# A fused layer norm, attention and gated MLP on one core: loading all x tiles at once, two tiles' statistics on ScalarE, and a last query group in two halves

## The chip, the core and the metric

The kernel runs on one core of one Trainium2 chip. Its metric is the device time of one execution in microseconds (us); the time before is the median of three runs. A further execution was taken by the hardware profiler, and its page and trace are what is read here. TensorE is called PE, VectorE DVE, ScalarE ACT, GpSimd POOL and SyncE SP. PEld is TensorE's weight load, which overlaps its matmuls.

## The reference

With x of 2048 rows and 1024 columns (bf16), 32 heads of 32 columns, and an MLP of 3584 hidden columns:

```python
xn = _layernorm(x)
qkv = (xn @ wqkv)                      # split into q, k, v of 32 heads
p = softmax(q k^T * 32 ** -0.5)        # per head, 2048 x 2048
s = (p v) @ wo
y = _layernorm(xn)
h = gelu_tanh(y @ w1 + b1)
g = silu(h @ w2 + b2)
out = x + s * g
```

## The kernel before

All work is described as operations for the five engines (PE, ACT, DVE, POOL, SP). A planner on the host (class _Plan) runs an event simulation with a cost for each operation, and so fixes, before launch, the order in which each engine takes its instructions. On the chip every engine takes its list in order and waits on semaphores. Priorities (the number at the end of a dve or act call, lower first), positions and due times of the dense PE work decide the planner's choices. ACT, DVE and PE are strictly in the planned order, so an instruction that waits holds up all that is behind it on its engine.

**Stages.** The rows of x are 16 tiles of 128. In the prologue each tile is loaded (load_x, L626), its mean and variance are computed, POOL raises the variance to the power -0.5 (L794), and DVE normalises it into one of four buffers (normalize, L748). Statistics are two BATCH_NORM_STATS2 (L785) and an aggregate (L787) on DVE, but for tile AT = 1, whose two passes (a copy and a square, each with an accumulator) run on ACT (L769) with three small DVE operations behind them. Tiles 0 to 3 are transposed on PE (tr_item, L733) and copied by ACT into xnT (L737); tiles 4 to 15 are transposed by DMA (L752). The first ten x tiles are loaded at once into buffers in hT; the other six follow when buffers come free (load_x with first[2n-5], L783).

From xnT the queries, keys and values of head group 0 are projected (q_item, k_item, v_item, at L617 as all plain matmuls). Query and key results of 256 columns are copied out of PSUM by DVE (L712) and by ACT (L722). Where PE has nothing else it runs idle matmuls on an identity (filler, L668).

**Attention.** There are eight head groups of four heads and eight query groups of 256 queries (qb) for each. A unit is one query group against 256 keys (kp): eight score matmuls for four heads side by side (L846) into four PSUM banks, then two exponentials of 128 x 1024 on ACT (L855) into a P buffer, of which there are ten in the steady state. Three pairs of banks serve the scores in turn. Value products (v_fn) and sums over keys are PE matmuls of 32 columns by 256 (L612); to save PE work DVE first adds P tiles pairwise (tree, pair_add: L872, L886) and PE sums the result with a matrix of ones. The quotient (L941 to L950) transposes the sums in blocks of 32, takes reciprocals, transposes them back, and multiplies the values.

**MLP.** In parallel, chunk after chunk of 256 rows: y is normalised and transposed by DMA, multiplied by w1 (L617, DVE adds the bias at L1022), then a gelu built from five DVE operations (L1034 to L1039, priority 3) and one tanh on ACT (L1037) over four hidden tiles at a time, then w2 (L617), a silu (tanh on ACT, L1064) and a store of g. The w2 items of a chunk start when the gelus they read are done.

**Ending.** In the last head group (own, w = HG - 1) each query group is followed by its output product with wo: per tile of 128 rows two pieces of 512 columns, eight accumulating matmuls each, then DVE multiplies by g (L1269) and adds x (L1272) and SP stores (L1299). For the last query group (late) the first seven of the eight matmuls run early (items in the queue "last"), DVE prepares xf from them (L1277, L1280), and after the quotient only the last matmul remains (items in lates, queue "fin"): piece 0 is finished on DVE (L1290, L1293), pieces 1 to 3 by a copy on ACT (L1285), a multiply and an add on DVE (L1287, L1293), and each is stored by itself (L1295).

```python
timing(pv, us, qb == NQB - 1)
quotient(pv, g, OTr[:, w, qb * 256:(qb + 1) * 256], [("OTr", w, qb)], dead, qb == NQB - 1, 0.5)
```

## Time and profile before

| What | Before |
|---|---|
| median of three runs | 1038.02 us (1036.59 to 1038.26) |
| the profiled execution | 1038.8 us, of which the span is 1037.0 us |
| mean granted TensorE clock | 0.998 |
| busy, share of the span | PE 97%, PEld 62%, DVE 91%, ACT 98%, POOL 1% |
| exponentials (L855) | 1004 records of 1024, 937.4 us busy, mean 1236 ns |
| DMA | 162 GB/s mean over the span, 167.99 MB |

The span runs from the first to the last instruction of the profiled execution; its time holds 1.8 us more, which lie around the span. Durations overlap where instructions are pipelined: an exponential lasts more than 1 us in its record and yet one begins every 0.92 us. Some matmul and activation records are missing. In the listings a line holds the start, the duration of the group, engine, source line, operation, output and inputs, the count, and in brackets the idle time before it with what ended it.

### The profile page before, as it was taken

What the parts mean: (1) busy time and instruction counts of PE and PEld (TensorE: products, weight loads), DVE (VectorE), ACT (ScalarE), POOL (GpSimd) and SP (SyncE); (2) the same over time, 40 slices, a digit from 0 to 9 for tenths busy, and PEclk for the clock granted to TensorE, in tenths of its full rate; (3) what the DMA queues carried; (4) which work ended last, traced back from release to release, by engine and by line L of the source; (5) the groups of instructions that cost most, each with busy time, mean ns of one, the idle gap of its engine ahead of it and who ended that gap; (6) DMA issues with size and microseconds to landing.
All of it is one profiled execution on the core that took longest, in us unless ns stands there. A gap on an engine that the chain in (4) does not pass through costs nothing.

```text
span 1037.0 us, 31480 instructions
## 1 busy us (share of the span) xinstructions
PE 1000.8 (97%) x14096; PEld 638.6 (62%) x14161; DVE 940.6 (91%) x1308; ACT 1017.2 (98%) x1094; POOL 11.5 (1%) x21
## 2 busy tenths in 40 slices
PE   8999999999999999999999999999999999899997
PEld 6656557666766567666666676666666665664443
DVE  7658999999889999997899989998999889877898
ACT  6999999999999999999999999999999999999996
POOL 2200000000000000000000000000000000000000
PEclk9999999999999999999999999999999999999999
DMA  7994655635665658456447576565365762784421
GB/s 204 166 234 118 173 166 165 191 108 147 192 186 167 168 152 227 129 147 194 136 129 189 146 215 172 159 179 161 104 160 161 212 175 70 230 249 137 135 79 52
DMA packets 318199, 167.99 MB, mean 162 GB/s; under 512 B 56688, under 2 KB 306032, under 8 KB 318064
## 3 DMA queue, kind: packets, MB, share of 16 engines
q1 hardware_dynamic: 318064, 165.98, 58.0%
q8 instruction: 111, 1.82, 0.8%
q14 instruction: 24, 0.20, 0.1%
HBM read 146.55 MB, written 12.06 MB: 153 GB/s over the span
## 4 chain that ended last, share of the span: by engine, by line
ACT 85%; PE 10%; DMA 2%; DVE 2%; issue 1%; SPq 0%; POOL 0%
ACT P L855 78%; PE ps L617 6%; ACT ut L1037 5%; PE ps L612 3%; PE ps L846 2%; DMA xnT<-gw 1%; ACT gw L1064 1%; DMA w2r<-in_B_w_dram 1%; DVE stats L785 1%; DMA hT<-in_A_x_dram 0%; DVE gw L748 0%; DVE hT L1293 0%; DVE V L690 0%; DVE hT L1287 0%; DVE mv L787 0%
## 5 line engine op out<-in xcount | busy, mean ns | idle before, releaser
L855 ACT ACTIVATE P<-ps 128x1024 bf16<-128x1024 f32 x1004 | 937.4, 1236 | 3.6 <-PE ps L846 3.4
L872 DVE TENSOR_TENSOR PA<-P 128x2048 bf16<-128x2048 bf16 x175 | 212.3, 1216 | 38.3 <-ACT P L855 37.7
L617 PE MATMUL ps<-yT,w1r 128*128 128x256 bf16 x1792 | 228.5, 273 | 1.0 <-DVE hT L1022 0.7
L617 PE MATMUL ps<-w2r,hT 128*128 128x256 bf16 x1792 | 223.2, 273 | 0.5 <-DMA w2r<-in_B_w_dram 0.2
L846 PE MATMUL ps<-QKT 32*128 32x256 bf16 x4096 | 203.3, 273 | 13.8 <-ACT P L855 10.9
L886 DVE TENSOR_TENSOR PR<-PR,PA 128x2048 bf16<-128x2048 bf16 x175 | 211.6, 1210 | 1.2
L617 PEld LDWEIGHTS ps<-yT,w1r 128*128 128x128 bf16 x1792 | 164.1, 98 | 54.5 <-issue 29.3
L617 PEld LDWEIGHTS ps<-w2r,hT 128*128 128x128 bf16 x1792 | 163.4, 98 | 50.0 <-issue 31.3
L846 PEld LDWEIGHTS ps<-QKT 32*128 32x128 bf16 x4096 | 60.7, 92 | 144.3 <-ACT P L855 137.3
L612 PE MATMUL ps<-P,V 128*32 128x256 bf16 x4016 | 137.2, 274 | 0.3 <-issue 0.3
L617 PE MATMUL ps<-xnT,wqk 128*128 128x512 bf16 (+1 forms) x511 | 119.1, 360 | 6.5 <-DMA xnT<-gw 2.4
L612 PEld LDWEIGHTS ps<-P,V 128*32 128x32 bf16 x4016 | 95.0, 96 | 31.8 <-issue 22.5
L617 PE MATMUL ps<-wv,xnT 128*128 128x256 bf16 (+1 forms) x576 | 87.1, 285 | 0.5 <-DMA xnT<-gw 0.2
L617 PEld LDWEIGHTS ps<-xnT,wqk 128*128 128x128 bf16 x560 | 49.6, 98 | 53.3 <-issue 14.1
L1022 DVE TENSOR_TENSOR hT<-ps,b1T 128x512 bf16<-128x512 f32 x112 | 76.5, 683 | 1.8 <-PE ps L617 1.1
L872 DVE TENSOR_TENSOR PR<-P 128x2048 bf16<-128x2048 bf16 x61 | 74.1, 1214 | 0.4 <-ACT P L855 0.2
L617 PEld LDWEIGHTS ps<-wv,xnT 128*128 128x128 bf16 x576 | 52.4, 98 | 24.1 <-issue 11.4
L1037 ACT ACTIVATE ut<-ut 128x2048 bf16<-128x2048 bf16 (+1 forms) x32 | 61.0, 1906 | 0.0
L702 DVE CAST QKT<-ps 128x512 bf16<-128x512 f32 x58 | 39.6, 683 | 1.3 <-PE ps L617 0.9
L941 DVE STREAM_TRANSPOSE nt<-ps 128x256 f32<-128x256 f32 x64 | 28.4, 443 | 12.7 <-PE ps L612 12.5
L1039 DVE TENSOR_TENSOR hT<-ut,hT 128x2048 bf16<-128x2048 bf16 (+1 forms) x32 | 34.5, 1079 | 0.2
L1034 DVE TENSOR_TENSOR ut<-hT 128x2048 bf16<-128x2048 bf16 (+1 forms) x32 | 34.5, 1079 | 0.1
(96 smaller groups left out, 549.5 us busy)
## 6 DMA issues: line engine op xcount, KB each, us to landing
w1r<-in_B_w_dram SPq DMA_DIRECT2D x112, 512.0 KB, 4.2
w2r<-in_B_w_dram SPq DMA_DIRECT2D x128, 448.0 KB, 4.6
hT<-in_A_x_dram SPq DMA_DIRECT2D x20, 256.0 KB, 3.9
wqk<-in_A_wqkv_dram SPq DMA_DIRECT2D x16, 256.0 KB, 3.9
yst<-in_A_x_dram SPq DMA_DIRECT2D x16, 256.0 KB, 4.4
g_scratch<-gw SPq DMA_DIRECT2D x32, 128.0 KB, 3.9
o_scratch<-ot SPq DMA_DIRECT2D x56, 64.0 KB, 3.4
xnT<-o_scratch SPq DMA_DIRECT2D x7, 512.0 KB, 6.6
```

Of the source, the lines that this page charges most:

```text
L612: ins = e.matmul(dst(j), lhsT=lhsT(j), rhs=rhs(j), start=start, stop=stop, tile_position=(0, 32 * j), skip_group_check=True)
L617: return e.matmul(dst, lhsT=lhsT, rhs=rhs, start=start, stop=stop, skip_group_check=True)
L702: dve(lambda e: e.tensor_copy(QKT[sl][:, which, tq * 512:(tq + 1) * 512], bank(it.bank)), c_ps(512), [], [(nm, sl, 2 * tq), (nm, sl, 2 * t ...
L846: ins = e.matmul(bank(b0[j], kk * 256, (kk + 1) * 256), lhsT=QKT[sl][32 * j:32 * j + 32, 1, kb * 128:(kb + 1) * 128], rhs=QKT[sl][32 * j:3 ...
L855: x = act(lambda e, h=h: e.activation(Pt[pi][:, 2 * h:2 * h + 2].rearrange("p j k q -> p (j k q)"), ps[:, pr[h] * 1024:(pr[h] + 1) * 1024] ...
L872: return dve(lambda e: e.tensor_tensor(dst[:].rearrange("p u j q -> p (u j) q"), src[:].rearrange("p u j k q -> p (u j) k q")[:, :, 0, :], ...
L886: return dve(lambda e: e.tensor_tensor(fl3(pr), fl3(pr), fl3(PA[i]), op=ALU.add), c_b16(2048), [("PA", i), tok], [tok], 3.2)
L941: dve(lambda e: e.transpose(nt_t[:], bank(pv.bank, 256, 512)), c_ps(256) + 120, [], [("nt",)], prio, pv)
L1022: dve(lambda e: e.tensor_tensor(hT[:, hs], bank(it.bank).rearrange("p (k t) -> p k t", k=2), b1T[:, 2 * pi:2 * pi + 2].unsqueeze(2).to_bro ...
L1034: dve(lambda e: e.tensor_tensor(u_, x_, x_, op=ALU.mult), c_b16(n), hs_, [("ut", ui)], 3)
L1037: act(lambda e: e.activation(u_, u_, ACT.Tanh, scale=GC), c_acts(n), [("ut", ui)], [("ut", ui)], 1)
L1039: dve(lambda e: e.tensor_tensor(x_, u_, x_, op=ALU.mult), c_b16(n), [("ut", ui)] + hs_, hs_, 3)
```

## The change

The change has two parts.

In the prologue all sixteen x tiles are loaded at once, the last six into buffers of the trees (PR) and of the MLP's input (yst); so the K weights of head group 1 and the first y tiles are loaded after the last tile's normalisation instead of after tile 9's and 11's. AT becomes (1, 3): tile 3's statistics run on ACT as well. The first queries and keys are projected for tile 0 and tile 1 separately (qk_first), into two banks at once, and tile 3's keys apart from tile 2's.

In the ending the last query group of the last head group is cut into two halves of 128 queries (half_unit: four units of 512 keys for each half, the same size of exponential; sums straight from P on PE, no tree; half_quotient). The output pieces of the first half are queued ahead (firsts, queue "fin0"), those of the second half stay last (lates). Query group 6 also takes its first seven output matmuls early. The gelu of the last MLP chunk is cut finer and gets higher priorities on DVE (1.4) and ACT (-1), the queries of the last head group are placed later, and the planner may run a transposition of the prologue between the matmuls of another item.

```diff
+            if use is None and S["do"] is not None and th < len(tq) and tq[th].chunks[0].left == 0 and tq[th].chunks[0].ready <= t:
+                heads["tr"] += 1
+                tq[th].k = 1
+                S["mode"] = "d"
+                commit(tq[th].chunks[0], t)
+                return
...
-        NTR, NWARM, NG0, AT = 4, 8, 3, 1
+        NTR, NWARM, NG0, AT = 4, 8, 3, (1, 3)
...
+        for i in range(2):
+            pr_flat = PR[i][:].rearrange("p u j q -> p (u j q)")
+            xst += [pr_flat[:, 0:1024], pr_flat[:, 1024:2048]]
+        xst += [yst_t[i][:] for i in range(2)]
...
-        for t in range(4, NXS):
+        for t in range(NTR, NT):
             load_x(t)
         load_v(0)
...
+            for lo, w in ((0, 128), (128, 128)) if n < 2 else ((0, 256),):
+                for dc in range(DC):
+                    def fn(e, b, dc=dc, lo=lo, w=w):
+                        at = n * 256 + lo
+                        return mm(e, bank(b, lo, lo + w), wqk[wk0][:, dc, :], xnT[:, dc, at:at + w], dc == 0 and lo == 0, dc == DC - 1)
+                    chunk(it, fn, Q256 if w == 256 else Q128, [("xnT", 2 * n + i, dc) for i in range(lo // 128, (lo + w) // 128)] + [("wqk", wk0)])
...
+        def qk_first():
+            it = _Item("pro", -0.001)
+            for lo, d0, d1 in ((0, 0, 8), (128, 0, 4), (128, 4, 8)):
+                for k, wi in ((0, wq0), (1, wk0)):
+                    for dc in range(d0, d1):
+                        def fn(e, b, dc=dc, lo=lo, k=k, wi=wi):
+                            return mm(e, bank(k or b, lo, lo + 128), wqk[wi][:, dc, :], xnT[:, dc, lo:lo + 128],
+                                      dc == 0 and lo == 0, dc == DC - 1)
+                        chunk(it, fn, Q128, [("xnT", lo // 128, dc), ("wqk", wi)], [("S", 0, 1)] if k else ())
+            dve(lambda e: e.tensor_copy(QKT[0][:, 0, 0:256], bank(it.bank, 0, 256)), c_ps(256), [], [("Q", 0, 0)], 0, it)
+            act(lambda e: e.activation(QKT[0][:, 1, 0:256], bank(1, 0, 256), ACT.Copy), c_act(256), [("S", 0, 1)], [("K", 0, 0)], -1)
...
+                if ts[0] in AT:
+                    a_ = ts[0]
                     for k, f, sc in ((0, ACT.Copy, 1.0 / D), (1, ACT.Square, D ** -0.5)):
-                        act(lambda e, k=k, f=f, sc=sc: e.activation(
-                            fl3(PA[0])[:, k * 1024:(k + 1) * 1024], xst[AT], f, scale=sc, accum_out=mv[:, AT, k:k + 1]),
-                            c_acts(1024) + 93, [XS(AT)], [("st", AT, k)], 1)
-                    dve(lambda e: e.tensor_tensor(lnp[:, AT:AT + 1, 2], mv[:, AT:AT + 1, 0], mv[:, AT:AT + 1, 0], op=ALU.mult), 65,
-                        [("st", AT, 0)], [("s2",)], 0.95)
-                    dve(lambda e: e.scalar_tensor_tensor(lnp[:, AT:AT + 1, 0], mv[:, AT:AT + 1, 1], EPS, lnp[:, AT:AT + 1, 2], op0=ALU.add,
-                                                         op1=ALU.subtract), 65,
-                        [("st", AT, 1), ("s2",)], [("ve", AT)], 0.95)
-                    dve(lambda e: e.tensor_tensor(mv[:, AT:AT + 1, 1], mv[:, AT:AT + 1, 1], lnp[:, AT:AT + 1, 2], op=ALU.subtract), 65,
-                        [("st", AT, 1), ("s2",)], [("mv", AT)], 1.1)
+                        act(lambda e, k=k, f=f, sc=sc, a_=a_: e.activation(
+                            fl3(PA[a_ // 2])[:, k * 1024:(k + 1) * 1024], xst[a_], f, scale=sc, accum_out=mv[:, a_, k:k + 1]),
+                            c_acts(1024) + 93, [XS(a_)], [("st", a_, k)], 1)
...
-                    if t >= NXS:
-                        load_x(t, [first[2 * n - 5]])
...
+            if n == 0:
+                pro_q.append(qk_first())
+            else:
+                if n < NG0:
+                    pro_q.append(q_item(n))
+                pro_q.append(k_item(n))
...
-            wk = load_qk(hg, 1, [first[9]] if hg == 1 else ())
+            wk = load_qk(hg, 1, [first[NT - 1]] if hg == 1 else ())
             wq = load_qk(hg, 0)
...
-            lst += [(x, "q", t) for t, x in enumerate((42, 46, 50, 54) if hg == HG - 1 else (42, 58, 72, 86))]
+            lst += [(x, "q", t) for t, x in enumerate((50, 52, 54, 56) if hg == HG - 1 else (42, 58, 72, 86))]
...
-                    [("yst", t2)], rate=390.0, extra=[first[11]] if c == 0 else ())
+                    [("yst", t2)], rate=390.0)
...
+            half = c == NCH - 1 and pi in (NW1 - 3, NW1 - 1)
+            if p % 4 != 3 and pi != NW1 - 1 and not (pi == 1 and c % 2) and not half:
                 return it
-            k = 2 if (pi == NW1 - 1 and p % 4 != 3) or (pi == 1 and c % 2) else 4
+            k = 2 if (pi == NW1 - 1 and p % 4 != 3) or (pi == 1 and c % 2) or half else 4
...
+            gp, ga = (1.4, -1) if c == NCH - 1 and pi >= 5 else (3, 1)
+            dve(lambda e: e.tensor_tensor(u_, x_, x_, op=ALU.mult), c_b16(n), hs_, [("ut", ui)], gp)
+            dve(lambda e: e.tensor_scalar(u_, u_, GA, 1.0, op0=ALU.mult, op1=ALU.add), c_b4(n), [("ut", ui)], [("ut", ui)], gp)
+            dve(lambda e: e.tensor_tensor(u_, u_, x_, op=ALU.mult), c_b16(n), [("ut", ui)] + hs_, [("ut", ui)], gp)
+            act(lambda e: e.activation(u_, u_, ACT.Tanh, scale=GC), c_acts(n), [("ut", ui)], [("ut", ui)], ga)
+            dve(lambda e: e.tensor_scalar_add(u_, u_, 1.0), c_b4(n), [("ut", ui)], [("ut", ui)], gp)
+            dve(lambda e: e.tensor_tensor(x_, u_, x_, op=ALU.mult), c_b16(n), [("ut", ui)] + hs_, hs_, gp)
...
+        for i in range(2):
+            after([("PR", i)], [XS(10 + 2 * i), XS(11 + 2 * i)])
+            after([("yst", i)], [XS(14 + i)])
...
+        def half_unit(hg, qb, a, kq, pv):
+            n = unit_n["n"]
+            unit_n["n"] += 1
+            sl, vs = hg % 2, vslot[hg]
+            m = slot_n["n"]
+            slot_n["n"] += 1
+            pi = (m - 16) % NP
+            b0 = [(4 * n + j) % 6 for j in range(4)]
+            q0 = qb * 256 + a * 128
+
+            def s_fn(e):
+                for kk in range(4):
+                    kb = 4 * kq + kk
+                    for j in range(4):
+                        ins = e.matmul(bank(b0[j], kk * 128, (kk + 1) * 128),
+                                       lhsT=QKT[sl][32 * j:32 * j + 32, 1, kb * 128:(kb + 1) * 128],
+                                       rhs=QKT[sl][32 * j:32 * j + 32, 0, q0:q0 + 128],
+                                       start=True, stop=True, tile_position=(32 * j, 0), skip_group_check=True)
+                return ins
+            pr = [b0[0] // 2, b0[2] // 2]
+            o = add("PE", s_fn, 300.0, 210, [("Q", sl, qb), ("K", sl, 2 * kq), ("K", sl, 2 * kq + 1)],
+                    [("S", k, h) for k in pr for h in range(2)])
+            plan.s_queue.append(o)
+            for h in range(2):
+                x = act(lambda e, h=h: e.activation(Pt[pi][:, 2 * h:2 * h + 2].rearrange("p j k q -> p (j k q)"),
+                                                    ps[:, pr[h] * 1024:(pr[h] + 1) * 1024], ACT.Exp, scale=SCALE),
+                        c_act(1024), [("S", pr[h], 0), ("S", pr[h], 1)], [("P", pi, h)], 0)
+            Ph = Pt[pi].rearrange("p j k (i q) -> p j (k i) q", i=2)
+
+            def v_fn(e):
+                for kk in range(4):
+                    ins = quad(e, lambda j: bankp(pv.bank, j, 0, 128), lambda j: V[:, vs, 4 * kq + kk, 32 * j:32 * j + 32],
+                               lambda j: Ph[:, j, kk, :], kq == 0 and kk == 0, False)
+                return ins
+
+            def o_fn(e):
+                for kk in range(4):
+                    ins = quad(e, lambda j: bankp(pv.bank, j, 256, 384), lambda j: ones[:], lambda j: Ph[:, j, kk, :], False, False)
+                return ins
+            ks = [("P", pi, 0), ("P", pi, 1)]
+            vc = add("PE", v_fn, 4 * Q128, TL, ks + [("V", vs, 2 * kq), ("V", vs, 2 * kq + 1)], [], item=pv)
+            oc = add("PE", o_fn, 4 * Q128, TL, ks + [("ones",)], [], item=pv)
+            return x, vc, oc
...
+        def half_quotient(pv, dst, W, extra, copied=False):
+            pq_ = -0.5 if copied else -2
+            if copied:
+                dve(lambda e: e.tensor_copy(nv_t[1][:, 0:128], bank(pv.bank, 0, 128)), c_ps(128), [], [("nv", 1)], -0.6, pv)
+            dve(lambda e: e.transpose(nt_t[:, 0:128], bank(pv.bank, 256, 384)), c_ps(128) + 120, [], [("nt",)], pq_, pv)
+            dve(lambda e: e.reciprocal(nr_t[:, 0:4], nt_t[:, 0:128].rearrange("p (b k) -> p b k", k=32)[:, :, 0]), 110,
+                [("nt",)], [("nr",)], pq_)
+            dve(lambda e: e.transpose(nt_t[:, 0:128].rearrange("p (b k) -> p b k", k=32),
+                                      nr_t[:, 0:4].unsqueeze(2).to_broadcast([128, 4, 32])), c_f32(128) + 20,
+                [("nr",)], [("nt",)], pq_)
+            if copied:
+                dve(lambda e: e.tensor_tensor(dst, nv_t[1][:, 0:128], nt_t[:, 0:128], op=ALU.mult), c_f32(128),
+                    [("nt",), ("nv", 1)], W, pq_, None, extra)
+                return
+            dve(lambda e: e.tensor_tensor(dst, bank(pv.bank, 0, 128), nt_t[:, 0:128], op=ALU.mult), c_ps(128),
+                [("nt",)], W, pq_, pv, extra)
...
+                if own and qb == NQB - 1:
+                    for h_ in range(2):
+                        pv = _Item("pv")
+                        us = [half_unit(w, qb, h_, kq, pv) for kq in range(4)]
+                        pv.chunks = [c for u in us for c in u[1:]]
+                        pv.mode = "v"
+                        pv.soon, pv.triggers = us[2][0], [us[3 - h_][0]] * 3
+                        plan.pv_queue.append(pv)
+                        half_quotient(pv, OTr[:, w, qb * 256 + h_ * 128:qb * 256 + (h_ + 1) * 128], [("OTr", w, qb, h_)], dead, h_ == 0)
...
-                if qb == NQB - 1:
-                    pv.chunks = [u[1] for u in us[:6]] + [tree_sums(g, pv, us[:6])]
-                    pv.chunks += [us[6][1], plain(us[6], pv), us[7][1], plain(us[7], pv)]
...
-                        late = qb == NQB - 1
+                        late = qb >= NQB - 2
+                        fin = qb == NQB - 1
...
+                            if fin:
+                                it.bank = 2 + 2 * t2 + nh
+                                if not t2:
+                                    it.due = 64 * HG - 2
+                            (plan.dense["wo"] if not fin else lates if t2 else firsts).append(it)
...
-                        xf = gw[:, i2 * 1024:(i2 + 1) * 1024].bitcast(F32)
+                        xk = (qb, i2)
+                        xf = (gw if fin else w1_flat)[:, i2 * 1024:(i2 + 1) * 1024].bitcast(F32)
...
-                        if i2:
+                            c_f32(512), [("xr", ri, nh)], [("xf", xk)], 2)
+                        if fin and i2 == 3:
...
+                        if fin:
+                          dma(f"osl{i2}", lambda e, xr=xr, tb=tb, sl_=sl_: e.dma_start(
...
-        plan.dense["fin"] = lates
+        plan.dense["fin0"], plan.dense["fin"] = firsts, lates
```

## The prediction

> **What bounds the kernel now.** I read the windows first (busy time of each engine in chosen stretches; the long ones in between are left out).
>
> ```profile
> core 0: us, PE busy (x) PEld busy (x) DVE busy (x) ACT busy (x) POOL busy (x), PEclk, DMA share, GB/s
> 13.00:20.00 7.00, 6.73 (x107) 5.49 (x100) 6.69 (x16) 6.01 (x8) 0.71 (x1) 1.00 0.49 115
> ...
> 200.00:900.00 700.00, 686.16 (x9606) 447.20 (x9644) 659.98 (x868) 699.93 (x745) 0.00 (x0) 1.00 0.59 163
> ...
> 1000.00:1026.30 26.30, 25.67 (x338) 11.56 (x338) 23.95 (x36) 26.29 (x29) 0.00 (x0) 1.00 0.11 39
> 1026.30:1037.00 10.70, 3.38 (x41) 1.40 (x31) 7.70 (x16) 1.57 (x3) 0.00 (x0) 0.81 0.21 74
> ```
>
> ScalarE (ACT) is busy for 699.93 of 700 us in the middle: the 1024 exponentials follow each other at about 0.92 us. So the time is: when the first exponential starts, plus ScalarE's idle time after that, plus its work, plus what follows the last exponential. The timeline gives the first and last of these, and the idle pieces between:
>
> ```profile
> 13.26 1.02 ACT L855 ACTIVATE P<-ps 128x1024 bf16<-128x1024 f32 x1 [0.50 <-PE ps L846]
> ...
> 23.07 0.38 ACT L722 ACTIVATE QKT<-ps 128x256 bf16<-128x256 f32 x1 [1.15 <-PE ps L617]
> ...
> 38.67 1.02 ACT L855 ACTIVATE P<-ps 128x1024 bf16<-128x1024 f32 x1 [0.92 <-PE ps L846]
> ...
> 64.68 3.77 ACT L855 ACTIVATE P<-ps 128x1024 bf16<-128x1024 f32 x4 [0.56 <-PE ps L846]
> 69.34 2.97 ACT L855 ACTIVATE P<-ps 128x1024 bf16<-128x1024 f32 x3 [0.89 <-PE ps L846]
> ...
> 1003.99 22.29 ACT L855 ACTIVATE P<-ps 128x1024 bf16<-128x1024 f32 x24
> ```
>
> Brackets hold the idle time and its releaser. The first exponential starts at 13.26. From there to 70 us ScalarE idles some 4.5 us: 1.15 for the keys of tiles 4 and 5, 0.92 for those of tiles 10 and 11, 0.56 and 0.89 where PE is late, the rest in small pieces. The last exponential ends at 1003.99 + 22.29 = 1026.28; 10.72 us follow to the end of the span.
>
> The chain of waits names what sets the idle pieces and the ending:
>
> ```profile
> 17.61 4.33 DMA xnT<-gw
> ...
> 31.57 6.24 DMA xnT<-gw
> ...
> 1027.12 0.46 DVE nt L941
> ...
> 1033.59 0.69 DVE hT L1293
> ```
>
> Transposes by DMA gate the keys; VectorE (DVE) alone carries the last 7 us, for four output pieces. The SP timeline shows what lay in front of the second DMA wait: four x tiles, at 27.92.
>
> ```profile
> 27.92 2.00 SPq L626 DMA_DIRECT2D hT<-in_A_x_dram  x4
> 30.21 4.15 SPq L752 DMA_TRANSPOSE xnT<-gw  x2
> ```
>
> **Prologue, step by step.** Tile 3's statistics leave VectorE: two BATCH_NORM_STATS2 (0.61 apart), an aggregate (0.21) and an add (0.15) go, three small operations at 0.07 to 0.15 come, so about 1.2 us. VectorE's chain from 6.02 to 16.64 has no gap but 0.23 behind POOL, so tiles 4 and 5 are normalised near 14.4, not 15.64. ScalarE gets two passes of 1.06 us, in its idle 1.45 us ahead of 7.95; tile 0's copy slips by some 0.7, and the idle 0.60 and 0.72 behind it absorb that. The first keys and queries are computed in half tiles, in two banks: after tile 1's copy only 8 of the 32 matmuls are left (18 of this size took 1.17 us at L668, 65 ns each, so 0.5) where 16 took 1.91, and the query copy no longer precedes the key copy. First exponential: near 12.7, 0.5 sooner. That is worth nothing unless the next gate moves too.
>
> The next gate is tiles 4 and 5, whose transposes were issued at 16.21 and landed at 21.94. Six x tiles (0.79 us of SP each, by 4.75 for six) now go out behind the first ten, so wv is issued near 13.7 instead of 8.97 (first used at 25.66, median landing 4.3: covered by 7 us), and the transposes can be issued near 14.6. But 1.57 MB more lies in front of them: the queue moved some 335 GB/s from 8 to 14 us and was then empty, so the added tiles keep it busy to 14 + 4.7 = 18.7. Lower end: no hindrance, 1.3 us sooner. Upper end: the transposes at 30.21 had 1.05 MB in front, took 7.6 us to land, and now 2.1 MB lies there: 14.6 + 7.6 + 1.05 MB / 335 GB/s = 25.3, 3.4 later. The nearest row is the 7.6 us by itself, since issue started long before: 22.2. I take +0.2. The in-order key copy at 23.07 holds up the eighth exponential, so this goes straight into the time.
>
> The Trainium skill has a rule against this part: DMA: Bandwidth & Descriptors, section Queues, rings and completion order, says that each DMA engine consumes a row's descriptors in ring order. The 7.6 us above agree with it; at its strictest the sum by it is rival A's.
>
> Later gates get better. No x tile lies in front of tiles 10 and 11 any more: with the median landing of these transposes, 3.0, or even 4.6, their keys come several us sooner, so the 0.92 idle goes: -0.9. The two PE pieces (1.45) come behind a stretch (40 to 60) in which PE is busy for 19.75 of 20 us, after waits for DMA at 21 and 37 (1.3 and 1.07). With tiles 10 to 15 earlier PE works in those holes; I take -0.9 of 0 to -1.45. The other moved loads (K weights of group 1, used near 70; the first y tiles, used at 47.00 behind POOL's pow, which ends at 45.0) wait for tile 15, normalised at 42.7 before and some 3 us sooner now; with 3.9 to 4.4 us to landing they stay covered; uncovered they delay the MLP, not ScalarE.
>
> Prologue: +0.2 - 0.9 - 0.9 = -1.6.
>
> **Ending.** Before: last exponential at 1026.28; first transpose 1027.12 (0.84 later); quotient ready 1028.75 (1.63); first product taken up 1029.33 (0.58); VectorE until 1034.28 (4.95); store and its landing to 1037.0 (2.72). After: only 128 queries are left. Value and sum matmuls 0.9. The quotient's three wide operations halve: from 0.42 at 256 to 0.68 at 512 columns a 128-column cut is worth 0.13 each, so 1.23. Product 0.58. VectorE has one scalar_tensor_tensor, one multiply and two adds, 0.61 + 0.61 + 0.34 + 0.69 = 2.25, in place of four pieces. Store 2.72. Sum 7.7: -3.0.
>
> What pays for it must fit ahead of 1026. VectorE in the last group: five tree operations go (5 x 1.21 = 6.1), the first half's quotient (1.4), its two pieces (2.7) and four times 0.27 come: 0.9 less than the 12.77 of 14.70 us now. Query group 6 takes its first seven products early, 4 x (0.68 + 0.69) = 5.5 more, against 9.3 idle us of VectorE from 940 to 1000. Without that cover each piece costs 1.4 in the tail. The first half's two pieces go to score banks 2 and 3, free only when the last unit but one is exponentiated, 1.8 us before the end of the last; their 2.7 on VectorE then reach past the 0.9 of waiting by 0.1 to 0.6: +0.2. PE: sums straight from P need 16 small matmuls a unit, about +1.4 net of the trees' own, scores +0.4: 1.8 more. The cover is a hole: with the last gelu stretched from 875.15 to 892.66 by VectorE's trees, PE ran idle matmuls (L668) and waits for 7.5 us:
>
> ```profile
> 882.43 0.40 PE L846 MATMUL ps<-QKT 32*128 32x256 bf16 x8 [0.68 <-ACT P L855]
> 882.76 1.18 PE L668 MATMUL ps<-ident 128*128 128x128 bf16 x18
> ```
>
> The early gelu (its VectorE operations ahead of the trees, its tanh first on ScalarE) lets the second MLP product start there, and the displaced work moves forward. If the hole stays, 1.8 us of products come behind the last exponential, half of it beside the quotient. Splitting the gelu costs ScalarE 2 x 0.94 - 1.79 = +0.1. The later queries of the last head group only shift within the same PE time; the gelu put first could delay trees, but P has ten slots, 18 us of exponentials: nothing.
>
> Scores of a half unit sit on the path: in the timeline the exponential follows the scores within 0.05 us. 16 matmuls of 128 columns replace 8 of 256. Same array time gives 0. If instead matmuls cannot follow faster than the densest long run shows (32 in 1.06 us, 25 ns), 15 x 25 + 272 = 0.65 against 0.40 is +0.25 a unit, +2.0 for eight. The eight now start within (0.40 - 0.27)/7 = 18 ns of each other on average, so the low end is nearer: +0.4.
>
> The Trainium skill states such a floor: TensorE: Matmul & The Clock Gate, section Wait — 56ns, not 53.3ns?, has start to start never below about 25 ns. The 18 ns here disagree; by the rule the ending would lose the 2.0 of rival B.
>
> Ending: -3.0 + 0.2 + 0.4 + 0.1 = -2.3.
>
> **Sum.** -1.6 - 2.3 = -3.9. The profiled execution took 1038.8 (span 1037.0 and 1.8 around it), 0.8 above the median of three, 1038.02. Its span becomes 1033.1; the median 1038.0 - 3.9 = 1034.1.
>
> **Rivals.** A: tiles 4 and 5 move only when the queue has drained, at 18.7; before, they began to move at 17.3 and landed 4.6 later, so 23.3: +1.4 instead of +0.2, and PE, which gets them late, wins back 0.5 instead of 0.9: prologue 0, ending -2.3, 1035.7. For it: the 31.57 row. Against: DMA is empty from 14 to 17 us. B: small matmuls step at 25 ns: scores +2.0 instead of +0.4, tail +0.4, so -3.9 + 2.0 = -1.9: 1036.1. Against: the 18 ns. C, slower: tiles 4 and 5 land so late that ScalarE, which must take their key copy in order, stands still with exponentials behind it. Every us of landing past 21.94 is one lost; with 2.3 from the ending it decides at 24.2 if nothing is won later. If the wv and x bytes delay the transposes twice (issue blocked by a full queue as well, so 25.3 plus the 1.35 to 2.1 of issuing each), they land near 27: +5 - 2.3 = +2.7, 1040.7. Against: SP kept issuing at 0.79 with the queue busy. D, the change does not do what it says: the gelu stays late, PE's rest lies behind the last exponential and the ending gives 1 less: within the range, counted in the forecast.
>
> **How the numbers follow.** Forecast 0.60, A 0.20, B 0.12, C 0.08. A difference of 0.2% (2.1 us) is about what can be told from no change. The forecast's own range, 1031.8 to 1035.7 (landing 1.3 sooner, all of 1.45 won; or the ending 1 to 1.5 less), lies below 1035.9: 0.60 faster. A and B straddle that bound: 0.12 + 0.08 faster, 0.07 + 0.03 same, 0.01 + 0.01 slower. C: 0.01 same, 0.07 slower. Together 0.80, 0.11, 0.09. Range: 1031.8 to 1037.2, leaving out C and the far ends of A and B.
>
> **What would show it.** Right: first exponential near 12.7; key copy of tiles 4 and 5 within 1 us of 23.07; no idle near 38 and less than 0.6 at 64 to 69; no L668 run near 885; from the last exponential to the end 7.9 us. Wrong: a key copy after 24.5; exponentials of the last group more than 0.95 apart; output pieces of the first half behind the last quotient.

## The result: 1040.05 us, 0.19% slower than before

The changed kernel takes 1040.05 us (median of 20 runs, 1037.86 to 1044.51), the kernel before 1038.17 (median of 20, 1036.51 to 1040.48). The ratio is 1.0019, 95% interval 1.0012 to 1.0026. The change was to win 3.9 us and lost 1.9. The range, 1031.8 to 1037.2, doesn't hold the result, and the spread has grown from 4.0 to 6.7 us. The profiled execution of the changed kernel took 1037.86 (span 1036.1): it is the fastest of the twenty, and 0.9 faster than the profiled execution before, so its trace shows less than the loss. A second profile, e12_after_again below, was of an execution of 1041.69.

The windows of the changed kernel:

```profile
core 0: us, PE busy (x) PEld busy (x) DVE busy (x) ACT busy (x) POOL busy (x), PEclk, DMA share, GB/s
13.00:20.00 7.00, 6.29 (x103) 4.82 (x99) 6.70 (x18) 7.00 (x10) 1.41 (x2) 1.00 1.15 292
...
200.00:900.00 700.00, 690.65 (x9616) 447.27 (x9617) 660.71 (x873) 699.42 (x746) 0.00 (x0) 1.00 0.59 165
...
1027.70:1036.10 8.40, 1.43 (x62) 0.76 (x50) 5.41 (x12) 0.62 (x2) 0.00 (x0) 0.84 0.19 62
```

The middle is as it was (ACT 699.42 of 700). The last stretch is shorter, 8.40 instead of 10.70. The first one looks better for ACT, 7.00 busy instead of 6.01, but the queue now moves 292 GB/s where it moved 115. ACT's timeline shows what follows from that:

```profile
13.26 1.02 ACT L883 ACTIVATE P<-ps 128x1024 bf16<-128x1024 f32 x1
...
25.60 0.38 ACT L735 ACTIVATE QKT<-ps 128x256 bf16<-128x256 f32 x1 [4.63 <-PE ps L628]
27.14 3.77 ACT L883 ACTIVATE P<-ps 128x1024 bf16<-128x1024 f32 x4 [1.16 <-PE ps L874]
...
49.10 0.38 ACT L735 ACTIVATE QKT<-ps 128x256 bf16<-128x256 f32 x1 [0.58 <-PE ps L628]
...
51.63 1.94 ACT L883 ACTIVATE w1r<-ps 128x1024 bf16<-128x1024 f32 x2 [0.24 <-PE ps L874]
...
1012.82 14.90 ACT L1187 ACTIVATE P<-ps 128x1024 bf16<-128x1024 f32 x16
```

The first exponential starts at the same 13.26. The key copy of tiles 4 and 5 comes at 25.60, behind 4.63 idle us, instead of 23.07 behind 1.15, and another 1.16 follow it. Eight exponentials precede it where seven did, so one of them, 0.92 us, is won back. The later idle pieces are small: 0.58 and 0.24 in place of 0.92, 0.56 and 0.89. The last exponential ends at 1012.82 + 14.90 = 1027.72, 1.44 later than before; the stretch behind it gives 2.3 back.

The SP timeline, the chain of waits, and PE's and DVE's timelines name the cause of the 4.63. Of the two PE lines the first is of the kernel before:

```profile
8.73 1.85 SPq L637 DMA_DIRECT2D PR<-in_A_x_dram  x4
10.63 0.95 SPq L637 DMA_DIRECT2D yst<-in_A_x_dram  x2
```

```profile
17.93 5.69 DMA xnT<-gw
...
1032.07 0.69 DVE hT L1400
```

```profile
21.98 1.70 PE L617 MATMUL ps<-xnT,wqk 128*128 128x256 bf16 x14 [1.30 <-DMA xnT<-gw]
```

```profile
23.67 3.08 PE L628 MATMUL ps<-xnT,wqk 128*128 128x256 bf16 x14 [3.97 <-DMA xnT<-gw]
```

```profile
27.45 0.42 DVE L723 CAST QKT<-ps 128x256 bf16<-128x256 f32 x1 [5.01 <-PE ps L628]
```

With the six x tiles in front, the second transpose is issued at 17.93 and lands 5.69 later, at 23.62, instead of 21.94. PE has nothing to do for 3.97 us. Then its 14 projections take 3.08 us, where the same 14 took 1.70 before. DVE, in order, waits 5.01 us for a query copy with the statistics of the later tiles behind it. Why 3.08? In narrow windows the granted clock (first figure behind POOL) falls and returns:

```profile
22.90:23.10 0.20, 0.00 (x0) 0.00 (x0) 0.00 (x0) 0.00 (x0) 0.00 (x0) 1.00 0.10 9
23.10:23.20 0.10, 0.00 (x0) 0.00 (x0) 0.00 (x0) 0.00 (x0) 0.00 (x0) 0.62 0.09 8
26.40:26.50 0.10, 0.10 (x3) 0.00 (x0) 0.00 (x0) 0.00 (x0) 0.00 (x0) 0.50 0.00 0
26.50:26.60 0.10, 0.10 (x2) 0.00 (x0) 0.00 (x0) 0.00 (x0) 0.00 (x0) 0.81 0.00 0
```

The clock is 1.00 or 0.50 in the slices around, so 0.62 in the slice from 23.10 means full clock for 24% of it, and the fall is at 23.12; 0.81 puts the return at 26.54. For 3.41 us PE has half its clock.

### The profile page after: what moved, and what is told of

Same layout as the page of the kernel before. It is cut to its first block, busy times and chain, and to the rows that moved or that the text cites. A ratio compares the mean times of both kernels' runs of the same rounds, so it can differ in the third digit from the quotient of the medians.

```text
span 1036.1 us, 31921 instructions
## 1 busy us (share of the span) xinstructions
PE 1006.8 (97%) x14339; PEld 638.2 (62%) x14339; DVE 940.1 (91%) x1320; ACT 1017.7 (98%) x1097; POOL 11.7 (1%) x21
## 4 chain that ended last, share of the span: by engine, by line
ACT 85%; PE 9%; DVE 3%; DMA 2%; issue 0%; POOL 0%; SPq 0%; DVEq 0%
ACT P L883 77%; PE ps L628 6%; ACT ut L1067 4%; PE ps L874 1%; DMA w2r<-in_B_w_dram 1%; PE ps L623 1%; ACT gw L1094 1%; ACT P L1187 1%; DVE PA L900 1%; DVE PR L914 1%; DVE stats L810 1%; DMA xnT<-gw 1%; ACT w2r L883 1%; DMA hT<-in_A_x_dram 0%; ACT hT L883 0%
## 5 line engine op out<-in xcount | busy, mean ns | idle before, releaser
L883 ACT ACTIVATE P<-ps 128x1024 bf16<-128x1024 f32 x988 | 923.5, 1241 | 1.9 <-PE ps L874 1.9
L900 DVE TENSOR_TENSOR PA<-P 128x2048 bf16<-128x2048 bf16 x173 | 210.1, 1217 | 33.9 <-ACT P L883 33.3
L914 DVE TENSOR_TENSOR PR<-PR,PA 128x2048 bf16<-128x2048 bf16 x173 | 209.4, 1212 | 1.2
L874 PE MATMUL ps<-QKT 32*128 32x256 bf16 x4032 | 200.3, 273 | 9.8 <-ACT P L883 7.7
L628 PE MATMUL ps<-xnT,wqk 128*128 128x512 bf16 (+2 forms) x584 | 132.8, 358 | 6.2 <-DMA xnT<-gw 4.0
L623 PE MATMUL ps<-P,V 128*32 128x256 bf16 (+1 forms) x4080 | 138.0, 272 | 0.0
```

Source lines behind the costliest of these rows:

```text
L623: ins = e.matmul(dst(j), lhsT=lhsT(j), rhs=rhs(j), start=start, stop=stop, tile_position=(0, 32 * j), skip_group_check=True)
L628: return e.matmul(dst, lhsT=lhsT, rhs=rhs, start=start, stop=stop, skip_group_check=True)
L874: ins = e.matmul(bank(b0[j], kk * 256, (kk + 1) * 256), lhsT=QKT[sl][32 * j:32 * j + 32, 1, kb * 128:(kb + 1) * 128], rhs=QKT[sl][32 * j:3 ...
L883: x = act(lambda e, h=h: e.activation(Pt[pi][:, 2 * h:2 * h + 2].rearrange("p j k q -> p (j k q)"), ps[:, pr[h] * 1024:(pr[h] + 1) * 1024] ...
L900: return dve(lambda e: e.tensor_tensor(dst[:].rearrange("p u j q -> p (u j) q"), src[:].rearrange("p u j k q -> p (u j) k q")[:, :, 0, :], ...
L914: return dve(lambda e: e.tensor_tensor(fl3(pr), fl3(pr), fl3(PA[i]), op=ALU.add), c_b16(2048), [("PA", i), tok], [tok], 3.2)
```

## Experiments

The expectations of the first four runs call T the theory that the loss is the later landing alone. From e5 on the theory is T1, or the clock theory: the x tiles in front make tiles 4 and 5 land later, PE runs dry, and its clock falls just when the projections come on which ACT and DVE wait in order; the loss is in the clock more than in the landing. Rivals: the later landing by itself; the queue; tile 3's statistics. All were compared with the kernel before on the same chip, whose median was 1038.04 for the first four, 1037.76 for the next four, 1037.62 for e9 to e12 and 1038.29 for the last three.

**e1_ending and e2_prologue: the change in two.** Each is the kernel before with one half of the diff: e1 has the half units, the split gelu, the queries at 50 to 56, the early products of query group 6; e2 all the rest.

```diff
# e1_ending, against before
-            lst += [(x, "q", t) for t, x in enumerate((42, 46, 50, 54) if hg == HG - 1 else (42, 58, 72, 86))]
+            lst += [(x, "q", t) for t, x in enumerate((50, 52, 54, 56) if hg == HG - 1 else (42, 58, 72, 86))]
+        def half_unit(hg, qb, a, kq, pv):
...
# e2_prologue, against before
-        NTR, NWARM, NG0, AT = 4, 8, 3, 1
+        NTR, NWARM, NG0, AT = 4, 8, 3, (1, 3)
-        for t in range(4, NXS):
+        for t in range(NTR, NT):
...
```

> The kernel before with the second part of the change alone (half query groups, early last gelu, group 6's products early). Theory T (the loss sits in the prologue, where the x tiles sent early hold up the transposes of tiles 4 and 5): about 2.3 us faster than before, since the profile after has 8.4 us behind the last exponential instead of 10.7. Rival B (small matmuls cost more than the trace let me think, and scores of half units come late): 0 to 0.5 us faster.

> The kernel before with the first part alone (all x tiles at once, tile 3's statistics on ACT, half-tile first projections). Theory T: 3 to 5 us slower than before (after is 2 slower although its ending gives 2.3), with the key copy of tiles 4 and 5 at 25 to 28 us and an idle time of 4 us or more before it. Rival B: within 1 us of before.

e1: 1036.12 (1035.03 to 1037.81), ratio 0.9982 [0.9973, 0.9991]: -1.9 us. e2: 1040.43 (1038.49 to 1045.72), ratio 1.0029 [1.0015, 1.0043]: +3.0. So the prologue loses more than the ending wins, and the prologue brings the spread.

**e3_x_behind and e4_x_all: the x tiles.** e3 is the changed kernel with tiles 10 to 15 sent once tile 5 is normalised, which puts them behind the transposes of tiles 4 and 5 on SP (transposes issued from 15.57, the x tiles from 18.29); e4 is the kernel before with nothing changed but that all x tiles are loaded at once (with the buffers and the later loads of K weights and y tiles that this brings).

```diff
# e3_x_behind, against the changed kernel
-        for t in range(NTR, NT):
+        for t in range(NTR, NXS):
             load_x(t)
...
+                if n == 3:
+                    for t in range(NXS, NT):
+                        load_x(t, [first[5]])
# e4_x_all, against before
-        for t in range(4, NXS):
+        for t in range(NTR, NT):
             load_x(t)
...
-                    if t >= NXS:
-                        load_x(t, [first[2 * n - 5]])
```

> The changed kernel, but x tiles 10 to 15 are issued behind the transpose of tile 4, no longer in one go behind the first ten; everything else of the change stays. Theory T: the key copy of tiles 4 and 5 comes back to 21 to 23 us, and the kernel is 3 to 5 us faster than the changed one, so 1.5 to 3 faster than before. Rival E (the new order of work on ACT, PE and DVE in the prologue costs the time by itself, whatever the queue carries): no better than the changed kernel, 1 to 3 us slower than before.

> The kernel before with nothing but x tiles 10 to 15 loaded at once behind the first ten (tile 3's statistics stay on DVE, projections as before, ending as before). Theory T: 2 to 5 us slower than before, the transposes of tiles 4 and 5 landing 2 us or more later than 21.9 us. Rival E: within 1 us of before, or faster by up to 2 us since no load lies in front of tiles 10 and 11.

e3: 1035.58 (1034.79 to 1038.58), ratio 0.9983 [0.9972, 0.9994], as expected. e4: 1038.62 (1036.69 to 1040.24), ratio 1.0005 [0.9995, 1.0016], a miss: 2 to 5 us slower was expected. PE's timelines, e3 and then e4:

```profile
21.96 1.81 PE L628 MATMUL ps<-xnT,wqk 128*128 128x256 bf16 x15 [1.78 <-DMA xnT<-gw]
```

```profile
23.50 3.17 PE L621 MATMUL ps<-xnT,wqk 128*128 128x256 bf16 x14 [2.58 <-DMA xnT<-gw]
```

With the tiles behind, the landing is at 21.91, PE waits 1.78 and keeps its clock (15 matmuls in 1.81). With the tiles in front, 2.58 us of waiting are followed by the half clock. ACT's idle time at this gate is 3.27 and 0.33 instead of 1.15; of these 2.4 us later gates give back half, as ACT is busy for 61.08 us from 13 to 80, and was for 62.27 before. So moving the x tiles is what makes the hole; by itself it did not lose the 3 us of e2, in which the hole is longer (4.13).

**e5_warm: the same landing with PE kept at work.** 60 idle matmuls are put right in front of the projections of tiles 4 and 5, at a planned cost of 0; nothing else is changed.

```diff
+            if use == "d" and dopen and dopen[1] is not None and getattr(dopen[0], "pre", 0):
+                f = self.add("PE", lambda e, b=dopen[1], n=dopen[0].pre: self.filler(e, b, n), 0.0, 0)
+                for x in bank_free[dopen[1]]:
+                    f.deps[x] = True
+                commit(f, start)
...
                 pro_q.append(k_item(n))
+                if n == 2:
+                    pro_q[-1].pre = 60
```

> The changed kernel, with 60 idle matmuls (3.9 us) put right in front of the first projection of tiles 4 and 5, where PE sat idle from 19.7 to 23.6; nothing else moves. Theory T1 (the late landing costs twice, since PE's granted clock falls to 0.50 in the wait and 14 projections then take 3.08 us instead of 1.70): key copy within 1.2 us of the landing, and 1 to 2 us faster than the changed kernel, so 0 to 1 slower than before. Rival (the clock does not matter, the landing does): within 0.5 us of the changed kernel, 2 slower than before.

```profile
19.07 4.30 PE L684 MATMUL ps<-ident 128*128 128x128 bf16 x74
23.95 1.70 PE L633 MATMUL ps<-xnT,wqk 128*128 128x256 bf16 x14 [0.58 <-DMA xnT<-gw]
```

1036.24 (1035.33 to 1037.65), ratio 0.9984 [0.9975, 0.9994]. The projections start even later than in the changed kernel (23.95), yet they take 1.70, the clock is 1.00 up to the last stretch of the kernel, and the time is 3.8 us less (3.6 by the two ratios), far more than expected. The spread shrinks from 6.7 to 2.3. Up to 45 us ACT, DVE and PE take the same instructions in the same order in both traces, but for the idle matmuls. This is the decisive run: the landing alone is not the loss.

**e10_prologue_warm and e9_at1_warm, e6_at1 and e13_at1_again.** e10 is e2 and e9 is e6 with the same 60 matmuls; e6 is the changed kernel with tile 3's statistics back on DVE, and e13 is e6 once more, for another profile.

```diff
# e6_at1, against the changed kernel
-        NTR, NWARM, NG0, AT = 4, 8, 3, (1, 3)
+        NTR, NWARM, NG0, AT = 4, 8, 3, (1,)
```

> The changed kernel, but tile 3's statistics are on DVE again (AT = (1,)), so tiles 4 and 5 are normalised and their transposes issued about 1.2 us later, behind a queue that has nearly drained. Theory T1 (issue into a full queue is what hurts, an earlier issue brings no earlier landing): 1 to 2.5 us faster than the changed kernel, so between 1.5 faster and the same as before. Rival (tile 3 on ACT is the useful part): 1 us or more slower than the changed kernel.

> e6_at1 again, for a second profile: its first was its fastest execution (1036.05, PE idle 2.27 us for tiles 4 and 5, clock 1.00 throughout). Clock theory: an execution of 1039 or more shows a granted clock of 0.50 somewhere between 23 and 35 us, the 14 projections at 3 us or more instead of 1.70, and the same order of work otherwise. Rival (the spread of e6_at1 comes from elsewhere, from transfers or later stages): clock 1.00 at 23 to 35 us in a slow execution too.

> The changed kernel with tile 3's statistics back on VectorE (as in e6_at1) and 60 idle matmuls right in front of the first projection of tiles 4 and 5 (as in e5_warm). Clock theory: what made e6_at1 slow and widely spread (1041.2, 1036.1 to 1044.4) is only that PE idles 2 to 4 us for tiles 4 and 5 and its clock falls in some executions more than in others; with PE kept at work the kernel comes to 1036.2 plus or minus 0.8 with all runs within 4 us, and the 14 projections take 1.70. Rival (VectorE's order: tile 3 on VectorE delays the statistics of later tiles and that costs in itself): it stays above 1039.

> The kernel before with the new prologue only (as in e2_prologue, 1040.4) and the 60 idle matmuls. Clock theory: 1037.2 to 1038.4, about the 1038.1 of before: the late landing of tiles 4 and 5 (23.6 instead of 21.9) costs some 1.5, the later gates win about that back, and the clock's 2.4 to 3 are gone. Rival (the late landing itself is the loss): 1039.5 or more, since the landing stays near 23.6.

e6: 1041.16 (1036.05 to 1044.42), ratio 1.0030 [1.0015, 1.0046]: a miss, it was to be faster than the changed kernel. Its profile was of its fastest execution, with PE idle for 2.27 us and no fall of the clock. e13 was an execution of 1037.62 and shows the same:

```profile
22.95 1.70 PE L628 MATMUL ps<-xnT,wqk 128*128 128x256 bf16 x14 [2.42 <-DMA xnT<-gw]
```

So 2.42 us of waiting left the clock at 1.00 here, while 2.58 in e4 did not; no execution of e6 near its median was profiled, so the slow execution that the expectation was about is not shown by a trace. But e9, which differs by the idle matmuls alone, gives 1037.41 (1036.18 to 1038.45), ratio 0.9998 [0.9989, 1.0006]: a little over the 1036.2 plus or minus 0.8 expected, and the spread of 8.4 us is 2.3. e10 gives 1038.18 (1036.56 to 1039.40), ratio 1.0001 [0.9993, 1.0010], as the clock theory said: without the clock's part the new prologue is neutral, and the clock's part is 1.0029 - 1.0001, some 2.9 us. e5 agrees: with the idle matmuls the whole change has 0.9984, and its ending alone, e1, 0.9982.

What the profiles leave out, the mean granted clock of every execution on record shows. One stretch of 3.41 us at half clock takes 0.0016 off it; the end of the kernel, where PE has next to nothing left, also runs at half clock, and adds 1.8 to 5.0 us of it in the profiles, which blurs the figure. Of the 121 executions of the kernel before in these comparisons 110 show 0.998 or 0.999. All 20 of the changed kernel show 0.993 to 0.997, all 12 of e2 too, and 11 of 12 of e6; the twelfth, at 0.999, is the one that was profiled. With the idle matmuls all 23 of e5 and e9 show 0.998 or 0.999, and 10 of 12 of e10. In e3 three executions are at 0.997 or lower, and they are its three slowest (1037.95 to 1038.58, the others 1034.79 to 1036.67).

**e12_after_again: a second profile of the changed kernel.**

> The changed kernel itself, for a second profile: the one at hand was its fastest execution (1037.9, median 1040.05). Clock theory: in an execution of 1040 or more the granted clock stays low for longer than the 3 us (23.6 to 26.5) seen in the fast one, the projections of tiles 4 and 5 take over 3.1 us, and ScalarE's idle time before 30 us is larger by the difference in time; after 80 us the two agree. Rival (contention of DMA queues): the landing of tiles 4 and 5 is what differs, at 25 or later instead of 23.6, at the same clock.

```profile
24.37 3.17 PE L628 MATMUL ps<-xnT,wqk 128*128 128x256 bf16 x14 [4.61 <-DMA xnT<-gw]
```

```profile
22.80:22.90 0.10, 0.00 (x0) 0.00 (x0) 0.00 (x0) 0.00 (x0) 0.00 (x0) 1.00 13.82 215
22.90:23.10 0.20, 0.00 (x0) 0.00 (x0) 0.00 (x0) 0.00 (x0) 0.00 (x0) 0.51 0.07 6
33.00:33.10 0.10, 0.10 (x8) 0.00 (x0) 0.00 (x0) 0.00 (x0) 0.00 (x0) 0.50 1.28 289
33.10:33.20 0.10, 0.10 (x5) 0.02 (x2) 0.00 (x0) 0.00 (x0) 0.00 (x0) 0.79 0.79 149
```

The landing is 0.7 later, as the rival has it in part, but the clock stays at half from 22.90 to 33.14: 10.24 us, three times 3.41. ACT's busy time from 13 to 80 us is 57.47, against 60.38 in the faster execution and 62.27 before; that is 2.9 of the 3.8 us between the two executions; the other 0.9 is lost elsewhere, though the two were expected to agree after 80 us. PE has work from 24.37 on, with one idle piece of 0.59 us, and still its clock comes back two periods later than in the first profile; why is not shown.

**e7_late and e11_behind_late: telling the planner the truth.** The planner thought that these transposes land soon after issue. e7 is the changed kernel with the planned landing of tiles 4 and 5 put 4 us later; e11 is e3 with the same, 3 us later.

```diff
-                    [("xnb", t % 4)], [("xnT", t, c) for c in range(DC)], prio=0, rate=300.0, occ=1300, lat=1000)
+                    [("xnb", t % 4)], [("xnT", t, c) for c in range(DC)], prio=0, rate=300.0, occ=1300, lat=5000 if t < 6 else 1000)
```

> The changed kernel, but the planner is told that the transposes of tiles 4 and 5 land 4 us later (5000 instead of 1000 ns behind the data), so that DVE's copy of the third queries no longer stands ahead of the statistics of tiles 8 to 11 and PE keeps itself busy until the data are there. The queue carries the same bytes in the same order. Theory T1: landing as late as in the changed kernel, but PE at full clock and DVE without its 5 us of waiting: 1 to 3 us faster than the changed kernel. Rival T0 (only the landing counts): within 0.7 us of it.

> The changed kernel with x tiles 10 to 15 sent behind tile 4's transpose (as in e3_x_behind, 1035.6) and with the planner told that the transposes of tiles 4 and 5 land 3 us later than it assumed (so that it puts other work ahead of their projections). If the two remedies add: the landing of 21.9 and a filled PE together give 1034 to 1035. If they are remedies for the same loss: 1035.2 to 1036, as each of them alone (1035.6 and 1035.2).

e7: 1035.22 (1034.19 to 1036.52), ratio 0.9975 [0.9965, 0.9984], the best of all and, at 4.6 us less than the changed kernel by the ratios, more than expected. The planner fills PE with idle matmuls and puts DVE's statistics ahead of the query copy:

```profile
18.41 3.63 PE L679 MATMUL ps<-ident 128*128 128x128 bf16 x62
22.56 1.59 PE L628 MATMUL ps<-xnT,wqk 128*128 128x256 bf16 x13 [0.52 <-DMA xnT<-gw]
```

e11 was to be 1034 to 1036 and took 1040.41 (1038.07 to 1041.94), ratio 1.0027 [1.0019, 1.0036]. In e3 too the x tiles stand in front of the transposes of tiles 6 and 7, which land at 28.68, but PE has other work and waits only 0.81 us for them. Here the planner has moved that work ahead, and the same hole opens one gate later:

```profile
28.91 0.61 PE L628 MATMUL ps<-xnT,wqk 128*128 128x256 bf16 x2 [5.69 <-DMA xnT<-gw]
```

Its clock is half from 26.29 to 33.12, 6.83 us, twice 3.41. Both expectations failed, and a hole with the half clock behind it is shown once more at another place. That planning tiles 6 and 7 later as well would mend it was not tried.

**e8_pe45: tiles 4 and 5 transposed on PE,** so that no DMA gates them.

```diff
-            if t >= NTR:
+            if t >= NTR + 2:
                 dma(f"tr{t}", ...
...
+            if n == 2:
+                pro_q += [tr_item(4), tr_item(5)]
```

> The changed kernel, but tiles 4 and 5 are transposed on PE and copied by ACT, as tiles 0 to 3 are, so no transpose of them stands in the queue behind the early x tiles. It costs ACT two copies (2 x 0.92 us). Theory T and T1: key copy of tiles 4 and 5 near 18 to 19 us, ACT idle before 30 us under 1.5 us instead of 6: 3 to 5 us faster than the changed kernel, so 1 to 3 faster than before. Rival (another gate, tiles 6 and 7, takes its place at once): 1 us or less faster than the changed kernel.

1037.07 (1034.77 to 1039.84), ratio 0.9996 [0.9985, 1.0008]: no gain over before that can be told, where 1 to 3 us were expected. The 4.63 is gone, but ACT pays two more copies of 1.02 each, and later idle pieces come in its place: 0.78, 1.49 and 0.68, all for PE, between 36 and 69 us.

**e14_warm_half and e15_late_warm: how much cover.** e14 has 30 instead of 60 idle matmuls; e15 has e7's planned landing and the 60 matmuls as well.

```diff
-                    pro_q[-1].pre = 60
+                    pro_q[-1].pre = 30
```

> The changed kernel with 30 instead of 60 idle matmuls ahead of the projections of tiles 4 and 5: they cover some 1.8 us, and some 2.2 of the 4 us of idle PE are left, behind them. If the length of the gap decides, with a bound between 1.8 (e3_x_behind, clock 1.00) and 2.6 (e4_x_all, 0.50): near the bound, a median between 1036.2 and 1038.5 with a spread of over 4 us. If any gap at this place costs in proportion to its length: half of e5_warm's gain, 1038.1 plus or minus 0.6. If work of PE shortly before the projections is enough: 1036.2 as with 60.

> The changed kernel with both remedies: the transposes of tiles 4 and 5 planned 4 us later (e7_late, 1035.2) and 60 idle matmuls ahead of their projections (e5_warm, 1036.2). Clock theory: e7_late had its PE covered already, so nothing is gained: 1035.0 to 1036.2 (the 60 matmuls can push the projections back by up to 1). Rival (some executions of e7_late are cold too): below 1034.8, with a spread under 2 us.

```profile
24.82 3.17 PE L633 MATMUL ps<-xnT,wqk 128*128 128x256 bf16 x14 [3.19 <-DMA xnT<-gw]
```

e14: 1039.40 (1037.10 to 1042.14), ratio 1.0009 [0.9998, 1.0019], outside all three expectations; of the first only the spread of over 4 us came (5.0). The transposes landed late, so 3.19 us were left open and the clock fell in the profiled execution; six of the twelve show a mean clock of 0.998 or 0.999, so it probably did not fall in all. It says that work shortly before the projections is not enough, and nothing on the bound. In e15 the planner's idle matmuls and the 60 added up:

```profile
19.24 6.99 PE L684 MATMUL ps<-ident 128*128 128x128 bf16 x122
26.07 1.58 PE L633 MATMUL ps<-xnT,wqk 128*128 128x256 bf16 x13
```

The projections wait for the cover instead of the data, and the time is 1037.79 (1036.84 to 1039.60), ratio 0.9999 [0.9990, 1.0007], 2.6 worse than e7. Both expectations were wrong; it does show that cover costs what it overshoots.

## Why the prediction was wrong, by its steps

**First exponential: right that it earns nothing by itself;** it did not move (13.26, not 12.7), because ACT copies another x tile (12.34 to 13.36) ahead of it. What the faster start gave is the one exponential more ahead of the key copy.

**The gate of tiles 4 and 5: mis-sized.** The step took +0.2, a landing at 22.2, as issue at 14.6 and the 7.6 us of the 30.21 row. The issue was at 14.99 and the landing 8.63 later, at 23.62, so +1.7. The prediction's own sign of being wrong, a key copy after 24.5, came with it. Rival A was near in size: a landing at 23.3, because the transposes move when the queue has drained, and the nothing that it left of the prologue's gain is what e10 measured. But part of the delay seems to be what rival C feared, an issue held up by a full queue. Issuing early bought little: the tile view shows that the first transpose held SP for 2.89 us, where the longest of the first two before took 1.34, so the second was issued at 17.93, 0.32 later than before, and it took 5.69 to land instead of 4.33.

```profile
L778 SPq DMA_TRANSPOSE xnT<-gw x4: 1233/1392/2892, 15.0 to 21.9; - x4
```

**What no term and no rival held: PE's own state behind the wait.** The step priced a late landing as one us of ACT for each us. It did not ask what PE does until then. By e10 against e2 the clock costs some 2.9 us, by e5 against the changed kernel 3.8; DVE's in-order wait with the statistics behind it is part of the same pile-up. Rival C's price, 1040.7, is near the result, but its point of decision, a landing past 24.2, was not reached in the first profile (23.62) and just passed in the second (some 24.3), and the larger part came by another way.

**Later gates: right.** The 0.92 for tiles 10 and 11 is gone, and 1.45 became 0.82: -1.55 against -1.8.

**Ending: right,** -2.3 forecast, -1.9 measured in e1. By the parts: half-unit scores +0.4 was too careful. PE's timeline has

```profile
1025.03 0.40 PE L1177 MATMUL ps<-QKT 32*128 32x128 bf16 x16 [0.16 <-ACT P L1187]
```

16 matmuls in the 0.40 of 8 before, so rival B is out. PE's hole at 882 was filled as planned, with 1.00 of it left:

```profile
882.08 0.38 PE L628 MATMUL ps<-w2r,hT 128*128 128x256 bf16 x2
883.46 0.40 PE L874 MATMUL ps<-QKT 32*128 32x256 bf16 x8 [1.00 <-ACT P L883]
```

so rival D, which would have lost 1 us by it, did not come. The tail is 8.4 instead of 7.9: DVE's last stretch was set at 2.25 for four operations, and takes 3.1 for five, from 1030.29 to 1033.36; the fourth of them is the addition at 1032.07 in the chain above, and another one follows it.

**The sum.** Ending -1.9, prologue without the clock 0, the clock +2.9: +1.0. Measured is +1.9 (+1.2 to +2.7); the intervals of e1 (-2.8 to -0.9) and e2 (+1.6 to +4.5) are wide enough for the difference.

**Open:** how many periods of half clock the median execution has, and what one costs. By single executions, none gives 1036.30 (e5), one 1037.86, three 1041.69, the last with a later landing: 1.6 to 1.9 us for each, so 1040.05 would be two. The clocks on record fit that only roughly: seven of the 20 executions show 0.997, as the profiled one with one period, and have a median of 1039.12; nine show 0.993 or 0.994, as the one with three, and have 1040.80. And one of those at 0.997 took 1043.07, so the clock is not all of the spread.

## What to carry to other kernels

When a change makes one engine wait longer for data, ask what state PE is in when the data comes: a hole of some us at full speed can be followed by several us at half speed, and everything that waits in order pays. Transfers sent early are not free because they are needed late. To send them behind the transfer that gates won, and to tell the planner the landing that the trace shows won; both together lost, because the hole moved to the next gate (e11), so look for the next hole after each remedy. Cover for a hole is cheap only up to the landing: 60 idle matmuls gained 3.8 us, and 60 more on top of the 62 that e7 already had lost 2.6.

## What the runs showed of the hardware

The half clock lasted 3.41 us in the changed kernel, in e2, e4 and e14, 6.83 in e11 and 10.24 in e12: one, two and three times the same period. It fell 3.4 us after PE's last work in the changed kernel (19.70 to 23.12), and 2.3 after in e4 (20.92 to 23.18), so no fixed wait sets it. The Trainium skill, TensorE: Matmul & The Clock Gate, section What's actually happening, has a free-running window of 3.413 us: an idle window brings half rate, a busy one full rate. The six durations agree with its length, and a free-running window, which can cut the same hole in different places, would fit the spread of e6 and of the changed kernel; no run here sets where it begins. That the window must be idle as a whole does not agree: in e4 PE had stood idle for only 2.3 us at the fall. The same page's section HAM oscillation — how this bites in real kernels asks for no idle gap over about 3.4 us; e4's 2.58 was enough for a fall and e13's 2.42 was not, so here the safe gap is shorter than that rule says.
